# Adding the rounding to a weight piece in two instructions of half the columns

## The chip, the cores and the metric

The kernel runs on one core of a Trainium2 chip. The metric is the device time of one execution in microseconds; the median of three runs before the change is 1360.98 us (1359.57 to 1361.94). A core has five engines that work side by side, each through its own queue in order: TensorE (PE, with its weight load PEld), VectorE (DVE), ScalarE (ACT), GpSimd (POOL) and SyncE (SP), which here issues the DMAs. They meet through semaphores.

## The reference

An attention block with normed queries and keys is followed by a two-layer network. The weights come as float64.

```python
q_n, k_n = rmsnorm(q, g_q), rmsnorm(k, g_k)          # (8, 12, 448, 64)
scores = (1/8) * q_n @ k_n.T
attn = softmax(scores)
x = (attn @ v) as (8*448, 768)
h = x @ w_in                                         # w_in (768, 2048), float64
out = (h - tanh(h)) @ w_out                          # w_out (2048, 768), float64
```

## The kernel before, in words

The 48 steps of attention (8 batches by 6 pairs of heads) are interleaved on TensorE with the matmuls of the network: `run(ns)` draws as much network work out of a generator as fits a gap between two stages of an attention step. The order of every queue is the order in which the Python code issues its instructions; nothing is reordered later. The network's products are formed by a scheme with seven products for eight blocks, which needs sums and differences of weight blocks.

Weights are float64 and are used as float32. They come in 32 pieces of 128 partitions by 768 values (`PIECES`; pieces 0 to 15 of w_in, 16 to 31 of w_out). A piece goes through these stages:
- load, by `weight_load` (lines 287 and 291, on SP): both 32-bit words of each value go to a raw buffer. The first eight pieces use space of the tile gT; from the ninth on there are three buffers named w_raw, so the load of a piece waits until the third piece before it has been finished.
- a, `round_weight_a` on ScalarE (lines 71 and 72): the high word becomes an absolute value in another scale; the low word is scaled in place.
- b, `round_weight_b` on VectorE (lines 78, 79 and 82): a clamp, a shift pair, and the sign bit.
- c, `round_weight_c` on GpSimd (line 90): the scaled low word is added to the bits, as an integer add, which does the rounding.

`weight` does stage a of the next piece and, through `settle`, b and c of the one before, then issues loads. It is called from the slots of the first batch and from inside the products of the first batch (`due` says which piece must be ready for which product). After every fourth piece of w_in, `combine_weights` lists four sums, which `combine` runs on VectorE (line 354) one at a time; they read whole pieces. `keep_weights` and `keep_w_out` store pieces and sums to DRAM for the later batches (lines 369 and 385, on SP). All 32 pieces have been through stage c after about 230 us.

Other lines named below: 140, 141 and 142 are the norm of a query and key pair (reduce and scale on VectorE, power on GpSimd); 454 and 452 scale the queries; 465 and 469 are transposes on TensorE; 567 the scores; 573 the exponentials; 694 the sums of the exponentials and 699 their reciprocal on VectorE; 621, 671 and 633 the products with v; 763 divides; 791 (GpSimd, sometimes VectorE) forms differences of x; 839 the matmuls of a product in the seven-product scheme; 906 to 922 combine products on ScalarE and VectorE; 886 and 887 are tanh and the subtraction of it (887 on GpSimd or VectorE); 1256 the matmuls of the second layer for the first batch, in which matmul f reads row block f of w_out, and a piece holds two such blocks, 384 columns each; 1049 (GpSimd) forms differences of g for later batches.

Of the kernel before, what the change touches and what calls it, by code (L numbers as in the profile page):

```python
# [13 lines left out]
ALU = mybir.AluOpType  # L14
# [72 lines left out]
def round_weight_c(nc, raw, dst):  # L87

    bits = dst.bitcast(I32)
    nc.gpsimd.tensor_tensor(out=bits, in0=bits, in1=raw[:, :, 0], op=ALU.add)  # L90


def fetch(nc, name, t, pair, in_order=False):
# [51 lines left out]
def bounded_path(tc, ctx, q, k, v, moe_w_in, moe_w_out, out, g_col, ident, ones, half_ones, neg_half, early):  # L145
# [192 lines left out]
    def finish_weights(to):  # L338
        while done[2] < to:
            round_weight_c(nc, raws.pop(done[2]), weight_dst(done[2]))  # L340
            done[2] += 1
            if done[2] % 4 == 0 and done[2] <= CF:
                combine_weights(done[2] // 4 - 1)
            keep_w_out(done[2] - 2)
# [1455 lines left out]
```

## Time and profile before

| | |
|---|---|
| median of three runs | 1360.98 us |
| the profiled execution | 1361.07 us |
| its span, first to last instruction | 1359.3 us |
| mean granted TensorE clock | 0.996 |
| PE, DVE, ACT, POOL busy | 1318.1, 956.4, 557.4, 762.9 us |
| L90 (32 instructions) | 17.1 + 9.2 + 41.0 us, 1.83 to 2.69 us each |
| L354 (16 instructions) | 0.95 to 2.61 us each |

The profile is of one execution. A line such as "L90 POOL ... 59.34 2.58" in a timeline is an instruction of line 90 on GpSimd that started 59.34 us after the span's start and took 2.58 us as recorded; the recorded time includes time in which the started instruction was held up. "A <- B" in the list of waits means that an engine sat idle before A until B ended. A busy share is an average over stages with different limits; what a change in one stage is worth is read from that stage.

### The profile page before, as it was taken

The page shows a single profiled execution, that of the slowest core. Times are in us where ns is not written, and L with a number is a line of the kernel's source. Part 1 is how long each engine was busy: PE and PEld are TensorE (multiplying, and loading weights), DVE is VectorE, ACT ScalarE, POOL GpSimd, SP SyncE. Part 2 cuts the span into 40 slices and gives each one's busy share as a digit, 9 for nine tenths or more (in the row PEclk, how much of TensorE's full clock was granted, in tenths as well). Part 3 has the DMA queues.
Part 4 walks back from the last instruction along what each step waited for, and adds up shares of the span by engine and source line. Part 5 has one row for each costly group of instructions (what it writes and reads, how often), then busy time and mean ns, then how long its engine had stood idle before and what let it go on. Part 6 is the DMA issues. An engine that isn't in the chain of part 4 may idle for free.

```text
span 1359.3 us, 29138 instructions
## 1 busy us (share of the span) xinstructions
PE 1318.1 (97%) x11336; PEld 1028.3 (76%) x11336; DVE 956.4 (70%) x1393; ACT 557.4 (41%) x1326; POOL 762.9 (56%) x559
## 2 busy tenths in 40 slices
PE   7988999999999999999999999999999999999996
PEld 3466854478998888687788787778787888699984
DVE  5999989756865677587887576768786668433553
ACT  7855654244343454445322446354512254211100
POOL 4756665347846246726698235843699153712760
PEclk9999999999999999999999999999999999999998
DMA  7878889879999766466555867475645865365544
GB/s 172 189 201 251 265 257 240 251 247 284 324 290 278 184 159 177 111 184 158 162 143 139 201 165 179 108 179 163 167 140 137 166 193 163 94 171 181 165 140 79
DMA packets 371687, 253.53 MB, mean 187 GB/s; under 512 B 282196, under 2 KB 310228, under 8 KB 371540
## 3 DMA queue, kind: packets, MB, share of 16 engines
q1 hardware_dynamic: 371536, 251.57, 67.2%
q8 instruction: 92, 1.51, 0.5%
q14 instruction: 55, 0.45, 0.1%
q10 hardware_dynamic: 4, 0.00, 0.0%
HBM read 205.23 MB, written 46.27 MB: 185 GB/s over the span
## 4 chain that ended last, share of the span: by engine, by line
PE 82%; DVE 10%; DMA 2%; SPq 2%; issue 1%; ACT 1%; POOL 1%; DVEq 0%; ACTq 0%; POOLq 0%
PE mm L839 35%; PE mm L1092 23%; PE sc L567 8%; PE sc L633 6%; PE mm L1256 5%; DVE xT L760 2%; DMA w_raw<-in_moe_w_in_dram 1%; PE sc L671 1%; DVE rows L611 1%; PE sc L621 1%; DVE rows L604 1%; DVE rows L598 1%; DVE sum_T L708 1%; SPq L125 1%; SPq L287 1%
## 5 line engine op out<-in xcount | busy, mean ns | idle before, releaser
L839 PE MATMUL mm<-xT,w_f 128*128 128x224 f32 x1296 | 264.0, 353 | 1.1 <-DVE s L910 0.7
L839 PEld LDWEIGHTS mm<-xT,w_f 128*128 128x128 f32 x1296 | 244.4, 190 | 7.2 <-issue 5.5
L567 PE MATMUL sc<-qT,kT 64*32 64x448 f32 (+1 forms) x3072 | 213.3, 498 | 2.7 <-ACT p_last L573 1.5
L839 PE MATMUL mm<-tt,w_f 128*128 128x224 f32 x1044 | 213.7, 356 | 0.6
L839 PEld LDWEIGHTS mm<-tt,w_f 128*128 128x128 f32 x1044 | 194.9, 190 | 18.9 <-issue 15.6
L521 POOL TENSOR_TENSOR rr_mine<-rr_mine,neg_half 128x28 f32<-128x28 f32 x33 | 160.6, 4866 | 2.8
L756 DVE TENSOR_TENSOR xT<-xT,sc 128x448 f32<-128x448 f32 x32 | 19.9, 621 | 177.6 <-PE sc L567 119.4
L1092 PE MATMUL mm<-u,w_f 128*128 128x224 f32 x672 | 136.5, 354 | 1.2 <-DVE sum_all L731 1.0
L887 POOL TENSOR_TENSOR gT<-s,th 128x448 f32<-128x448 f32 x44 | 55.8, 1270 | 144.9 <-ACT th L886 141.7
L1092 PE MATMUL mm<-gT,w_f 128*128 128x224 f32 (+1 forms) x480 | 133.0, 429 | 3.1 <-DVE acc L1099 3.0
L1092 PEld LDWEIGHTS mm<-u,w_f 128*128 128x128 f32 x672 | 126.1, 190 | 8.2 <-POOL u L1049 3.8
L567 PEld LDWEIGHTS sc<-qT,kT 64*32 64x32 f32 x3072 | 70.8, 106 | 70.1 <-issue 51.7
L1092 PEld LDWEIGHTS mm<-gT,w_f 128*128 128x128 f32 x480 | 90.2, 190 | 40.6 <-issue 34.2
L633 PE MATMUL sc<-p,v_nat 64*32 64x448 f32 x1120 | 110.5, 536 | 0.0
L1092 PE MATMUL mm<-g,w_f 128*128 128x224 f32 (+1 forms) x360 | 99.5, 428 | 1.1 <-DVE acc L1099 1.1
L723 ACT COPY sum_g<-sum 32x14 f32<-32x14 f32 x280 | 56.3, 201 | 105.8 <-DVE sum L715 100.1
L573 ACT ACTIVATE p<-sc 128x448 f32<-128x448 f32 x132 | 71.7, 543 | 50.3 <-PE sc L567 42.4
L887 POOL TENSOR_TENSOR g<-s,th 128x448 f32<-128x448 f32 x24 | 30.3, 1265 | 108.5 <-ACT th L886 93.6
L1092 PEld LDWEIGHTS mm<-g,w_f 128*128 128x128 f32 x360 | 67.9, 190 | 28.1 <-issue 26.2
L1256 PE MATMUL mm<-gT,w_out 128*128 128x448 f32 x192 | 74.3, 542 | 0.0
L142 POOL TENSOR_TENSOR rr<-rr,neg_half 112x8 f32<-112x8 f32 (+1 forms) x30 | 49.1, 1667 | 32.7 <-DVE rr L141 32.3
L1049 POOL TENSOR_TENSOR u<-gT 128x448 f32<-128x448 f32 x48 | 59.1, 1252 | 11.1 <-PE mm L1092 11.1
(196 smaller groups left out, 2424.0 us busy)
## 6 DMA issues: line engine op xcount, KB each, us to landing
w_f<-w_in SPq DMA_DIRECT2D x196, 384.0 KB, 3.4
w_f<-w_inner SPq DMA_DIRECT2D x63, 512.0 KB, 3.5
w_f<-w_out SPq DMA_DIRECT2D x42, 512.0 KB, 3.8
w_raw<-in_moe_w_out_dram SPq DMA_DIRECT2D x16, 768.0 KB, 5.5
w_in<-w_out SPq DMA_DIRECT2D x21, 384.0 KB, 5.2
qk_nat<-in_q_dram SPq DMA_DIRECT2D x132, 56.0 KB, 2.9
qk_nat<-in_k_dram SPq DMA_DIRECT2D x132, 56.0 KB, 2.3
g<-w_out SPq DMA_DIRECT2D x14, 512.0 KB, 4.7
```

The source lines that it names most:

```text
L142: nc.gpsimd.tensor_tensor(out=r, in0=r, in1=neg_half[:rows], op=ALU.pow)
L521: nc.gpsimd.tensor_tensor(out=mine, in0=mine, in1=neg_half[:, :1].to_broadcast([P, 2 * NJ]), op=ALU.pow)
L567: nc.tensor.matmul(tiles[h][i * BL : (i + 1) * BL, :n], lhsT=kT[r, c * P + at : c * P + at + BL], rhs=qT[r, first : first + n], start=True ...
L573: nc.scalar.activation(p[:, h, c if c < 2 else 0, :], tiles[h][:, :n], AF.Exp, scale=1.0 if rr is None else rr[:, 0, 2 * c + h : 2 * c + h ...
L633: nc.tensor.matmul(av[g][i * BL : (i + 1) * BL, :S], lhsT=v_nat[keys, h, c, m * BL : (m + 1) * BL], rhs=p[keys, h], start=first, stop=True ...
L723: nc.scalar.copy(out=acc[h * BL : (h + 1) * BL, g], in_=part[g * BL : (g + 1) * BL, h * NJ : (h + 1) * NJ])
L760: nc.vector.tensor_tensor(out=x[rows], in0=x[rows], in1=rs, op=ALU.mult)
L839: nc.tensor.matmul(bank[:, f * HS : (f + 1) * HS], lhsT=w[:, c * width + f, :], rhs=moving[p](c), start=(first and f == 0 and c == 0), sto ...
L887: eng.tensor_tensor(out=g[:, rows, cols], in0=h, in1=th, op=ALU.subtract)
L1049: nc.gpsimd.tensor_tensor(out=u[:, half], in0=a[:, half], in1=z[:, half], op=ALU.subtract)
L1092: nc.tensor.matmul(bank[:, :n], lhsT=w(i), rhs=mv, start=(first and i == 0), stop=(i == len(moving) - 1), skip_group_check=not first,)
L1256: nc.tensor.matmul(bank[:, :S], lhsT=w_out_row(f, n // HC)[:, n % HC * P : (n % HC + 1) * P], rhs=g[:, f, :], start=(f == 0), stop=(f == C ...
```

## The change

Stage c of a piece is issued as two integer adds instead of one, the first over columns 0 to 383 and the second over columns 384 to 767 of the same piece. Values, buffers and the order of all other instructions are the same.

```diff
 def round_weight_c(nc, raw, dst):
 
     bits = dst.bitcast(I32)
-    nc.gpsimd.tensor_tensor(out=bits, in0=bits, in1=raw[:, :, 0], op=ALU.add)
+    half = bits.shape[1] // 2
+    for part in (slice(0, half), slice(half, 2 * half)):
+        nc.gpsimd.tensor_tensor(out=bits[:, part], in0=bits[:, part], in1=raw[:, part, 0], op=ALU.add)
```

## The prediction

> **What bounds the kernel now.** I read the page's head first (PE 97% busy), then the waits of PE, then the busy times by stretch, then the timelines of DVE and POOL. The add on line 90 runs 32 times, all of them between 32.2 and 230.4 us, so only that part matters. Busy time by stretch, columns start:end, length, then PE, PEld, DVE, ACT, POOL busy with instruction counts, granted clock, DMA share, GB/s:
>
> ```profile
> 66.00:72.00 6.00, 5.54 (x80) 2.92 (x84) 5.81 (x9) 2.64 (x6) 5.38 (x6) 0.72 0.94 210
> 72.00:124.00 52.00, 43.26 (x440) 33.49 (x433) 50.95 (x67) 26.63 (x48) 30.68 (x16) 1.00 0.82 234
> 124.00:236.00 112.00, 111.96 (x896) 73.81 (x895) 100.95 (x126) 67.39 (x123) 69.06 (x42) 1.00 0.85 248
> ```
>
> From 72 to 124 us DVE is busy 50.95 of 52 us and PE only 43.26; after 124 PE has no gap (111.96 of 112). What PE waited for between 58 and 126 us (total us, times, longest):
>
> ```profile
> PE mm L839 <- DVE s L908: 4.0, 2, 2.5
> PE sc L465 <- DVE rs L699: 3.9, 2, 2.6
> PE mm L465 <- DVE rs L699: 1.9, 1, 1.9
> PE mm L839 <- DVE s L918: 0.8, 1, 0.8
> PE mm L694 <- DVE xT L763: 0.5, 1, 0.5
> ```
>
> All 11.1 us are waits for DVE, at 64.05, 67.2, 83.9, 90.0, 104.1, 117.7 and 121.0 us; the last ends at 123.61. DVE works its queue in order and has hardly a gap from 54 to 124 us, so a microsecond taken from it before the reciprocal L699 at 122.0 is a microsecond of the kernel, and nothing after 124 or before 54 is. (PE has no gap from 45 to 64 either.)
>
> Part of DVE's busy time is blocking. The timeline around the first piece with sums (start us, us, instruction), POOL and DVE lines together:
>
> ```profile
> 56.04 0.97 POOL L791 TENSOR_TENSOR tt<-xT,tt 128x224 f32<-128x224 f32 x1 [0.56 <-DVE xT L763]
> 56.52 0.91 DVE L79 TENSOR_SCALAR w_out<-w_out 128x768 int32<-128x768 int32 x1
> 56.97 0.98 POOL L791 TENSOR_TENSOR xT<-xT 128x224 f32<-128x224 f32 x1
> 57.46 1.40 DVE L82 SCALAR_TENSOR_TENSOR w_out<-gT,w_out 128x768 int32<-128x768 int32 x1
> 57.91 1.47 POOL L791 TENSOR_TENSOR tt<-xT,tt 128x224 f32<-128x224 f32 x1
> 58.79 1.41 DVE L354 TENSOR_TENSOR w_out<-w_out,w_out 128x768 f32<-128x768 f32 x1
> 59.34 2.58 POOL L90 TENSOR_TENSOR w_out<-w_out,gT 128x768 int32<-128x768 int32 x1
> 60.23 2.51 DVE L354 TENSOR_TENSOR w_out<-w_out,w_out 128x768 f32<-128x768 f32 x1
> 62.66 0.67 DVE L140 TENSOR_REDUCE rr<-n 112x8 f32<-112x512 f32 x1
> ```
>
> Undisturbed, L79 takes 0.56, L82 0.96, L354 0.95, a 224-column POOL subtraction 0.66 and L90 1.83 us. Here each instruction is long by just the rest of the other engine's. The second L354 takes 2.51 because L90 runs till 61.92: its own 0.95 us begin at 61.79. The engines take turns, each handover some 0.12 us before the other's recorded end. Decisive for the change: the POOL subtraction at 56.97 has no wait of its own and stands directly behind the one before, yet L79, waiting since 56.52, got in between.
>
> **What the Trainium skill says.** "SBUF — State Buffer", section "SBUF: two separate sides": DVE and GpSimd share a port pair as an exclusive lock, held for the whole instruction; the loser blocks fully. Its section "Who interferes with whom" says that DVE instructions with two SBUF inputs or in a 2-port mode contend, tensor_reduce and those with one SBUF input don't. The trace agrees: L78, L79, L82 and L354 are stretched (0.56 to 2.10, 0.95 to 2.61), L763 and L908, with one input in PSUM, never (0.39, 0.62). "GPSIMD Engine Reference", section "Instruction dispatch": each instruction pays a dispatch, an indirect call of tens of cycles; the trace prices it below. "TensorE: Matmul & The Clock Gate", section "What's actually happening": the clock halves after an idle window of about 3.4 us that doesn't start with the kernel. Here the granted clock was 0.50 between 68 and 70 us, after the stalls at 64 and 67; the 32 matmuls of L694 then took 3.1 us instead of 1.65.
>
> **The change, part by part.** It replaces each 768-column add by two of 384. Nothing else moves on any engine. GpSimd has 32 instructions more; the second half has almost never a wait of its own. Consumers of a whole piece (sums L354, the reload of the raw buffer on SP, keeps) now wait for the second half; matmuls wait for the half they read.
>
> Length of a half: 224 columns take 0.66 us, 448 take 1.14 (L887), 768 take 1.83: 2.15 ns a column and 0.17 us fixed. A half is 0.17 + 384 x 2.15 ns = 1.00 us; with the 0.04 us that back-to-back POOL instructions overlap, a pair is 1.97, 0.14 more than 1.83. Over 32 pieces that is 4.5 us of POOL time, hidden by POOL's idle time: 21 us in 72 to 124, 43 us in 124 to 236.
>
> What it does to DVE: a contending DVE instruction now waits for at most one half, and the second half waits behind it. That gains only where the DVE instruction after it doesn't contend and hides the second half; where contending ones follow each other, DVE waits for the second half too. I go through the ten pieces in the bound stretch, letting the two take turns with a handover of 0.12 us:
> - 49.6: L141 (a tiny tensor_scalar, stretched to 0.77) waits for a pair that ends 0.12 later: -0.12.
> - 59.3 and 71.4, the same pattern: L354 starts when the first half ends, 0.82 earlier; the second half runs beside the reduce L140, but its tail holds L141 by 0.14 to 0.17: +0.68 each.
> - 83.7: beside L699, which doesn't contend; L78 waits for the later end: -0.14.
> - 87.7 and 91.3: L79/L82 and L78/L79 follow each other; DVE waits once for each half: +0.07 and +0.08.
> - 95.8: L354 0.81 earlier, second half beside L887, tail holds L78: +0.50.
> - 101.8: four L763 beside it, nothing contends: 0.
> - 108.7: L78 then L79, and the POOL subtraction L887 behind: +0.09.
> - 113.5: L354 0.82 earlier, second half beside L140, then the second L141 meets L887: +0.60.
> Sum: -0.12 + 1.36 - 0.14 + 0.15 + 0.50 + 0 + 0.09 + 0.60 = 2.44 us by L699 at 122.0. The piece at 121.4 delays nothing before that.
>
> Can PE and the others follow? Two DVE instructions come close to waiting for PE: L914 (its matmuls end 104.08, it starts 104.66) and L908 (117.7 and 118.54). PE's own shift there is 1.17 and 1.75, against DVE's 1.75 and 2.44, so they tie with 0 and 0.15 us left; no loss, but no more gain. The second halves end up to 1.0 us later. The reload on SP at 98.30 waits for such an end; its data are used by ACT at 105.26, 3.4 us after landing. Queued behind it on SP are a store and the q and k rows for a later pair. The matmuls closest to an add are those of the piece at 187.97: they need its first half at about 190.8 and its second at 191.6; the halves end at about 189.3 and 190.6 (before: 190.13). After 124 us nothing is gained and, with these margins, nothing lost.
>
> Unknowns, from both sides. Handover between the halves: full, 2.44; never, ten times 0.14 lost, +1.4. I take full, because of 56.97. L141's holding: nothing, gain up to 2.9; a whole half at 59 and 71, gain 1.6. Fixed cost of a half: 0.1 to 0.3 us, gain from 2.9 down to 1.7.
>
> Against the profiled execution (1361.07 us, span 1359.3, 1.8 around it): 1361.07 - 2.44 = 1358.6. That execution is 0.09 above the median 1360.98, so the same number stands for both: 1358.6 us, -0.18%. A measurement of this kernel can tell about 0.2% (2.7 us) from no change; the shown runs spread over 2.4 us.
>
> **Rivals.** (a) The clock halves after the last stall. The stalls at 117.7 and 121.0 stay about 4 us together less 0.7; before, the gate didn't fall there. The halved clock at 68 us was hidden by the next stall; behind 123.6 nothing hides it: about 1.5 us (3.1 - 1.65), gain left 0.9, 1360.1. Against: one stall in seven did it. (b) The second half holds the pair against the waiting DVE instruction, so the change doesn't do what it does on paper: +1.4, 1362.4. Against: 56.97 and 57.91. (c) Slower: the weight stream becomes the bound. From 124 us SP waits long for L90 before reloading the three raw buffers, and ACT for the DMA. If each of the four turns of a buffer up to the piece at 187.97 loses 0.9 us and its matmuls wait, with a lead of 2.9 us (its bits were ready at 185.08) and 1.5 us more, it decides from 4.4 us on; at twice 0.9 a turn, 7.2 - 4.4 = 2.8 lost, and with nothing gained 1363.8. Against: four turns at 0.9 are 3.6. (d) More is given back: L141 isn't held, the fixed cost is below 0.17: 3.3 us, 1357.7.
>
> **How the numbers follow.** The main case, 2.44 with bounds 1.6 to 2.9: 0.58; (d) 0.20; (a) 0.12; (b) 0.05; (c) 0.05. With 0.8 us of scatter in a difference of medians, somewhat under half of the main case and most of (d) lie beyond 2.7 us: faster 0.45. Slower is (c) with part of (b): 0.07. The rest, 0.48, is within 0.2%. The main case alone reaches from 1357.3 to 1360.0; 8 times in 10 with the others 1356.9 to 1361.0.
>
> **What would show it.** Right: L90 twice 1.0 us; the L354 at 60.2 at some 1.7 us instead of 2.51; PE's stalls for DVE at about 8.7 us instead of 11.1; the last of them ends near 121.2; the rest from there as long as before. Wrong: L354 still 2.5 us (b), a clock of 0.5 beyond 121 us (a), waits of PE on L90 after 124 us (c).

## The result, and the profile after

The changed kernel takes 1357.89 us (median of 18 runs, 1356.19 to 1361.06), the kernel before, run beside it, 1361.43 (18 runs, 1359.57 to 1363.98). The ratio is 0.9973, 95% interval 0.9966 to 0.9980: 3.7 us faster (2.7 to 4.6), or 0.27%. The forecast was a gain of 2.4 us, just under what can be told from no change. The time lies in the predicted range and in the main case's own range (1357.3 to 1360.0), but the measured gain is larger than the working gave: 2.4 lies below its interval. The profiled execution took 1356.19 us, with a span of 1354.4 against 1359.3 before.

The head of the page after, busy time of each engine:

```profile
span 1354.4 us, 29206 instructions
PE 1317.9 (97%) x11336; PEld 1029.0 (76%) x11336; DVE 949.1 (70%) x1393; ACT 556.9 (41%) x1326; POOL 775.1 (57%) x591
```

DVE has as many instructions as before (1393) and is busy 7.3 us less (956.4 before): its instructions do the same, so what went is time in which they were held. POOL has the 32 instructions more and is busy 12.2 us longer, where the working priced the 32 at 4.5. Most of the rest is time in which halves were held in their turn (up to 1.87 us each where the shortest took 1.00).

The same three stretches as in the prediction (start:end, length, PE, PEld, DVE, ACT, POOL busy with instruction counts, granted clock, DMA share, GB/s), of the kernel after:

```profile
66.00:72.00 6.00, 5.54 (x113) 2.84 (x116) 5.80 (x9) 3.35 (x8) 5.39 (x6) 1.00 1.04 231
72.00:124.00 52.00, 45.10 (x419) 36.51 (x410) 49.39 (x67) 28.28 (x50) 33.40 (x25) 0.97 0.84 236
124.00:236.00 112.00, 112.00 (x885) 72.48 (x884) 98.18 (x129) 64.95 (x120) 77.01 (x61) 1.00 0.88 251
```

From 72 to 124 us PE is busy 45.10 us instead of 43.26, partly because the clock, 1.00 there before, was at 0.5 for 3.4 us from 91.8 us on. What PE waited for between 45 and 126 us (total, times, longest), after:

```profile
PE sc L467 <- DVE rs L701: 3.9, 2, 2.3
PE mm L841 <- DVE s L910: 2.5, 1, 2.5
PE mm L467 <- DVE rs L701: 1.0, 1, 1.0
PE mm L841 <- DVE rs L701: 0.5, 1, 0.5
PE mm L696 <- DVE xT L765: 0.5, 1, 0.5
```

That is 8.4 us instead of 11.1, again all for DVE (lines after the edited one are numbered two higher). The last of these stalls ends at 120.83 instead of 123.61 us. This is the predicted picture, 8.7 us and about 121.2, a little better.

The piece that the prediction took for its example, DVE and POOL lines of the timeline after, together (start us, us, instruction):

```profile
58.90 3.11 DVE L356 TENSOR_TENSOR w_out<-w_out,w_out 128x768 f32<-128x768 f32 x2
59.48 3.43 POOL L92 TENSOR_TENSOR w_out<-w_out,gT 128x384 int32<-128x384 int32 x2
61.94 0.67 DVE L142 TENSOR_REDUCE rr<-n 112x8 f32<-112x512 f32 x1
62.65 0.29 DVE L143 TENSOR_SCALAR rr<-rr 112x8 f32<-112x8 f32 x1
```

Consecutive like instructions stand on one line. The two sums take 3.11 us together and not 1.41 + 2.51; taken singly they are 1.43 and 1.65 us, the second from 60.36 on. The reduce follows at 61.94 instead of 62.66. This execution stood 0.12 us behind before it, so the second sum gave 0.84 us (0.82 in the working), and the tiny L143, held to 0.29 us by the second half, took 0.12 of that back. The two halves run from 59.48 to 62.91, where the whole add ran to 61.92: GpSimd now ends later and VectorE earlier. The prediction's price of a half, 1.00 us, is the shortest of the 40 halves of pieces w_out read against the raw buffer (1.001 us, median 1.032, longest 1.866, the long ones held by VectorE).

How VectorE's gain builds up, comparing the two profiled executions instruction by instruction, in us:

| piece at (before) | predicted | measured |
|---|---|---|
| 49.6 | -0.12 | +0.18 |
| 59.3 | +0.68 | +0.72 |
| 71.4 | +0.68 | +0.70 |
| 83.7 | -0.14 | -0.15 |
| 87.7 | +0.07 | +0.13 |
| 91.3 | +0.08 | +0.16 |
| 95.8 | +0.50 | +0.53 |
| 101.8 | 0 | 0 |
| 108.7 | +0.09 | +0.14 |
| 113.5 | +0.60 | +0.65 |
| sum | 2.44 | 3.06 |

The execution after was 0.30 us late on VectorE before any of these pieces, so that at the reciprocal L699 (122.0 us) VectorE is 2.78 us ahead. TensorE is ahead by the same 2.78 us at its last stall, and by 3.04 us at its last matmul (1343.33 us instead of 1346.37). The other 1.85 us of the 4.9 by which the spans differ lie behind the last matmul, in a tail of 11.07 us instead of 12.91. That tail is 9.5 to 13.3 us in the profiled executions of all the kernels below, without order (12.01 and 12.91 where nothing is cut, 13.16 and 9.53 where pieces are cut), so I don't count it as the change's.

### The profile page after: what moved, and what is told of

Read it like the earlier page. It is cut to its first block, busy times and chain, and to the rows that moved or that the text cites. A ratio compares the mean times of both kernels' runs of the same rounds, so it can differ in the third digit from the quotient of the medians.

```text
span 1354.4 us, 29206 instructions
## 1 busy us (share of the span) xinstructions
PE 1317.9 (97%) x11336; PEld 1029.0 (76%) x11336; DVE 949.1 (70%) x1393; ACT 556.9 (41%) x1326; POOL 775.1 (57%) x591
## 4 chain that ended last, share of the span: by engine, by line
PE 84%; DVE 9%; DMA 2%; SPq 2%; issue 1%; ACT 1%; POOL 1%; DVEq 0%; ACTq 0%
PE mm L841 36%; PE mm L1094 23%; PE sc L569 9%; PE sc L635 6%; PE mm L1258 5%; DVE xT L762 1%; PE sc L673 1%; PE sc L623 1%; SPq L955 1%; PE mm L673 1%; DVE rows L613 1%; DMA w_f<-w_in 1%; DVE rows L606 1%; DVE rows L600 1%; DMA w_f<-w_inner 0%
## 5 line engine op out<-in xcount | busy, mean ns | idle before, releaser
L1051 POOL TENSOR_TENSOR u<-gT 128x448 f32<-128x448 f32 x48 | 58.8, 1247 | 11.1 <-PE mm L1094 11.1
```

Of the source, the lines that this page charges most:

```text
L1051: nc.gpsimd.tensor_tensor(out=u[:, half], in0=a[:, half], in1=z[:, half], op=ALU.subtract)
```

## The experiments

The question: does the whole gain come from the ten pieces in VectorE's stretch, by the turns that the two engines take, as the prediction says (the theory)? Or does part of it come from the other 22 pieces, or from something else (the rival)? All kernels have this edit in common, with another list of cuts in each:

```
-def round_weight_c(nc, raw, dst):
+def round_weight_c(nc, raw, dst, n):
     bits = dst.bitcast(I32)
-    nc.gpsimd.tensor_tensor(out=bits, in0=bits, in1=raw[:, :, 0], op=ALU.add)
+    cuts = cuts_of(n)
+    for lo, hi in zip(cuts, cuts[1:]):
+        nc.gpsimd.tensor_tensor(out=bits[:, lo:hi], in0=bits[:, lo:hi], in1=raw[:, lo:hi, 0], op=ALU.add)
```

Here n is the piece, 0 to 31. The ten pieces of the table above are 2 to 11. The ten of the experiments are 3 to 12: without the piece at 49.6, and with the one at 121.4, which by the prediction's reading delays nothing before the reciprocal. Lines behind it are numbered six higher than before (L96 is the add, L360 the sums, L705 the reciprocal). "VectorE" below is by how much its reciprocal at 122.0 us came earlier than in the profile of the kernel before; it is negative where that came later, and two executions differ in it by up to 0.7 us with nothing cut. All gains in time come from the ratio to the kernel before on the same chip, whose medians were 1362.05, 1361.80 and 1361.92 us in the three groups of runs.

### Only the ten pieces in halves

```
+    return (0, 384, 768) if 3 <= n <= 12 else (0, 768)
```

> Only the ten pieces of the stretch in which DVE bounds (pieces 3 to 12, adds between 59 and 124 us) are added in two halves, the other 22 in one instruction. Theory (the gain is DVE time given back in that stretch alone): the last stall of PE for DVE ends some 2.8 us earlier than before and the whole is 2.5 to 3.7 us faster, as with all pieces split. Rival (the finer waits of the later pieces, for matmuls and reloads, give part of it): under 1.5 us.

Measured: 1359.65 us, ratio 0.9983 (0.9974 to 0.9993), 2.3 us faster (1.0 to 3.5). VectorE 2.90 us. The step from instructions to VectorE's lead holds.

### All but the ten pieces

```
+    return (0, 768) if 3 <= n <= 12 else (0, 384, 768)
```

> The other half of the change: pieces 0 to 2 and 13 to 31 in two halves, pieces 3 to 12 in one instruction. Theory: within 0.7 us of before, PE's stalls for DVE at about 11 us as before. Rival (later pieces count): 1 to 2 us faster. Second rival (the later ends of the second halves cost something that the whole change hides): 1 us slower.

Measured: 1359.92 us, ratio 0.9990 (0.9981 to 0.9998), 1.4 us faster (0.3 to 2.6). VectorE -0.13 us, and TensorE's stalls up to 126 us sum to about what they were before (11.3 and 11.1 us). So there is a gain elsewhere, and the rival has a part. The two parts, 2.3 and 1.4, add up to the 3.7 of the change.

### Only four pieces in halves

```
+    return (0, 384, 768) if n in (3, 4, 8, 11) else (0, 768)
```

> Only pieces 3, 4, 8 and 11 are added in two halves: those behind whose add DVE has an instruction that does not contend (a reduce, or a subtraction out of PSUM). Theory (a split gains only where such an instruction hides the second half): 2.6 us by the last stall, nearly all of the gain of all ten. Rival (any split add gives DVE an earlier turn): four tenths of it, about 1.1 us.

Measured: 1359.99 us, ratio 0.9983 (0.9975 to 0.9992), 2.3 us faster (1.1 to 3.4). VectorE 2.55 us. The four pieces at which a sum met the add, and a reduce or other instruction that doesn't contend stood behind it, bring nearly all of the 2.90 that all ten bring, and not the four tenths (about 1.1) of the rival. The gain isn't spread evenly over the pieces.

### The add of the ten pieces left out

```
+    return (0,) if 3 <= n <= 12 else (0, 768)
```

> The add is left out for pieces 3 to 12, so these weights lack the rounding by the low word. What the whole adds cost DVE: theory (blocking by the shared port) 9.5 us of DVE time by the last stall; PE's stalls for DVE were 11.1 us in all, so the whole is 7 to 9.5 us faster, less where DVE or PE then wait for each other. Rival (POOL's adds only happen to stand beside DVE's long instructions): under 3 us, and the sums still up to 2.5 us each.

Measured: 1351.12 us, ratio 0.9918 (0.9905 to 0.9930), 11.2 us faster (9.5 to 12.9). VectorE 9.85 us. This is the whole price of these ten adds, though GpSimd was idle for 21 us from 72 to 124 us. What TensorE waited for between 45 and 126 us in this kernel:

```profile
PE sc L471 <- DVE rs L705: 2.0, 2, 1.1
PE mm L845 <- DVE s L914: 0.6, 1, 0.6
PE mm L700 <- DVE xT L769: 0.5, 1, 0.5
PE mm L471 <- DMA qk_nat<-in_q_dram: 0.4, 1, 0.4
```

3.5 us are left of 11.1. So most of what TensorE waits for in this stretch is VectorE held by the add of its neighbour. Of the 9.85 us on VectorE the change gives back 2.78, under a third.

### Quarters

```
+    return (0, 192, 384, 576, 768)
```

> All pieces in four adds of 192 columns (0.58 us each). Theory (turns; the gain per handover shrinks since each part adds its fixed 0.17 us and the rest of the parts meets the next contending instruction): DVE is 3.2 us earlier at the last reciprocal than before, 0.4 more than with halves; whole 3 to 4 us faster than before. Rival (the finer the better in proportion): 5 us or more.

Measured: 1358.04 us, ratio 0.9974 (0.9964 to 0.9985), 3.5 us faster (2.0 to 4.9). VectorE 2.81 us, no more than with halves; 3.2 was expected, and the scatter of 0.7 is larger than that difference. What VectorE waited for between 54 and 124 us shows a wait that the arithmetic of turns didn't have:

```profile
DVE w_out L360 <- POOL w_out L96: 1.0, 1, 1.0
DVE w_f L360 <- POOL w_f L96: 0.5, 1, 0.5
```

In the timeline, the add and the sum that waits for it (eight quarters of two pieces stand on one POOL line):

```profile
85.38 6.74 POOL L96 TENSOR_TENSOR w_out<-w_out,gT 128x192 int32<-128x192 int32 x8 [1.54 <-ACT qT L479]
...
88.90 1.33 DVE L360 TENSOR_TENSOR w_out<-w_out,w_out 128x768 f32<-128x768 f32 x1 [1.04 <-POOL w_out L96]
```

A sum reads whole pieces. Each part lets one more of VectorE's instructions through, so the last part ends later, and the sum behind it stands idle for that end. The first reader of the whole piece sets a limit to finer cuts here.

### Unequal parts

A quarter of the columns first, and a quarter last:

```
+    return (0, 192, 768)      # small_first
+    return (0, 576, 768)      # big_first
```

> All pieces in two adds of 192 and 576 columns. Theory (turns): the waiting DVE instruction comes in earlier, but the long second part (1.41 us) outlasts the instruction that should hide it and holds the next contending one: 1.9 us by the last stall, 0.9 less than equal halves. Rival (only the time to the first handover counts): 0.4 us at each of ten pieces more than halves, 5 us or more.

> All pieces in two adds of 576 and 192 columns. Theory (turns): 1.3 us by the last stall. Rival (the number of instructions counts, not where the cut is): as with equal halves, 2.8 us.

Measured: small first 1358.65 us, ratio 0.9978 (0.9972 to 0.9985), 3.0 us faster (2.0 to 3.8), VectorE 1.29 us (1.95 counted from 58.8 us on, where this execution stood 0.66 behind); big first 1358.73 us, 0.9977 (0.9969 to 0.9985), 3.1 us faster (2.0 to 4.2), VectorE 1.65 us. On VectorE both are worse than halves. The waiting instruction is held by the first part, and the tiny one after the reduce by what is left of the second part, so neither part may be long. In the times the three can't be told apart.

### The sums later in the slot

Halves as in the change, and the sums moved from the end of a slot to behind the norm's reduces and the reciprocal:

```
         if has(s):
             totals(s, mm_bank())
+        combine(2)
...
             weight(s + 2)
-        combine(2)
```

> Halves, and in the first slots the two sums on DVE stand behind the reduces and the reciprocal of the next pair instead of right behind the sign step, so that the add runs beside instructions that do not contend. Theory (turns): DVE is 3.6 us earlier than before by the last stall, 0.9 more than with halves; whole 3.3 to 4.5 us faster than before. Rival (the sums only move their wait, since the small scale steps between the reduces are held instead): no better than halves, 2.8 us.

Measured: 1356.69 us, ratio 0.9965 (0.9952 to 0.9978), 4.8 us faster than before (3.0 to 6.5), the fastest version here that leaves nothing out (five runs). Beside the changed kernel's own interval (0.9966 to 0.9980) that isn't a safe difference. VectorE 3.41 us. DVE and POOL lines of its timeline at the example piece:

```profile
58.80 0.70 DVE L146 TENSOR_REDUCE rr<-n 112x8 f32<-112x512 f32 x1
59.39 1.99 POOL L96 TENSOR_TENSOR w_out<-w_out,gT 128x384 int32<-128x384 int32 x2
59.54 0.89 DVE L147 TENSOR_SCALAR rr<-rr 112x8 f32<-112x8 f32 x1
60.35 0.67 DVE L146 TENSOR_REDUCE rr<-sq 128x8 f32<-128x512 f32 x1
61.44 1.56 DVE L705 RECIPROCAL rs<-mm 128x224 f32<-128x224 f32 x1
62.92 2.22 DVE L360 TENSOR_TENSOR w_out<-w_out,w_out 128x768 f32<-128x768 f32 x2
```

The add now runs beside the reduces, which don't contend (0.70 and 0.67 us there); a pair takes 1.99 us, and of VectorE's instructions only the tiny L147 is held (0.89 us for 8 columns, the second one 0.36). The sums, which read two inputs in SBUF, come when the add is over. The reciprocal, for which TensorE waits, starts at 61.44 and not behind the sums.

### The same order with whole adds

The move of the last experiment, and:

```
+    return (0, 768)
```

> The sums behind the reduces and the reciprocal as in the run with halves, but every add in one instruction. Theory (turns): a whole add holds the small scale step between the reduces for 1.2 us and ends only there, DVE 0.5 us earlier than before at the last reciprocal, so the whole within 1 us of before: the new order needs the halves. Rival (the order alone brings it): 1.5 us or more.

Measured: 1360.79 us, ratio 0.9995 (0.9985 to 1.0004): no difference. VectorE came 0.32 us later than before. At the example piece the tiny instruction alone now takes what the sums were spared, and the sums don't run undisturbed either (timeline, DVE):

```profile
60.19 1.75 DVE L147 TENSOR_SCALAR rr<-rr 112x8 f32<-112x8 f32 x1
...
64.24 2.52 DVE L360 TENSOR_TENSOR w_out<-w_out,w_out 128x768 f32<-128x768 f32 x2
```

So the order alone brings nothing that can be measured. That it pays with an add in halves fits VectorE's 3.41 us against 2.78, but neither that nor the difference in time is clear of the scatter.

### Cuts chosen piece by piece

The sums later as above; quarters for pieces 3 and 4, thirds for 8, halves for 6, 7, 10 and 11, the rest whole.

```
+    return {3: (0, 192, 384, 576, 768), 4: (0, 192, 384, 576, 768), 6: (0, 384, 768), 7: (0, 384, 768), 8: (0, 256, 512, 768), 10: (0, 384, 768), 11: (0, 384, 768)}.get(n, (0, 768))
```

> The sums behind the reduces, and cuts where they pay: quarters for pieces 3 and 4, halves for 6, 7, 10 and 11, thirds for 8, the rest whole. Theory (turns): DVE 4.4 us earlier than before at the last reciprocal, whole 4 to 5.5 us faster. Rival (with more parts the sums wait for the last part, as with quarters everywhere): no better than halves with the sums later, 3.4 us at the reciprocal.

Measured: 1358.04 us, ratio 0.9977 (0.9968 to 0.9985), 3.2 us faster (2.0 to 4.4), VectorE 3.64 us, where 4.4 was expected. At the example piece, four quarters hold both tiny L147 (0.48 and 0.50 us, undisturbed 0.17), where two halves held the first for long and the second less (0.89 and 0.36). The late pieces are whole here, and the gain in time is no more than VectorE's.

### Nothing cut, and only the late pieces

A control with the loop in place and every piece whole, and the nineteen pieces behind VectorE's stretch in halves:

```
+    return (0, 768)                                     # same_again
+    return (0, 768) if n <= 12 else (0, 384, 768)       # split_late
```

> Every add in one instruction, as in the kernel before: what the comparison gives for no change. Both theories: ratio 1.000 within 0.001, DVE at the last reciprocal within 0.4 us. It says how much of the 1.4 us that the split of pieces 0 to 2 and 13 to 31 alone measured is more than that.

> Only pieces 13 to 31 in two halves. Theory (nothing can be gained after PE has caught up with DVE): within 0.7 us of before. Rival (the later pieces do give 1 us or more, by the finer waits of the matmuls and reloads): 1 to 2 us faster, and a place after 126 us in the trace where PE runs ahead of before.

Measured: the control 1361.59 us, ratio 1.0003 (0.9994 to 1.0012); the late pieces alone 1359.83 us, ratio 0.9984 (0.9976 to 0.9993), 2.2 us faster (1.0 to 3.3), while VectorE was 0.37 us later. So there is a second gain, clear of the control's interval around no change, and it lies behind 124 us, where the prediction had none.

Part of it shows between 215 and 240 us. SyncE's load of a raw piece, ScalarE's first step on it and the exponentials behind that, and TensorE's scores, in the control:

```profile
220.39 0.37 SPq L297 DMA_DIRECT2D w_raw<-in_moe_w_out_dram  x1
226.96 0.95 ACT L71 ACTIVATE w_out<-w_raw 128x768 f32<-128x768 f32 x1 [4.30 <-DMA w_raw<-in_moe_w_out_dram]
229.07 0.78 ACT L579 ACTIVATE p_last<-sc,rr 128x224 f32<-128x224 f32 x2
228.57 1.98 PE L573 MATMUL sc<-qT,kT 64*32 64x448 f32 x16
```

With the late pieces in halves:

```profile
220.06 0.37 SPq L297 DMA_DIRECT2D w_raw<-in_moe_w_out_dram  x1
225.75 0.95 ACT L71 ACTIVATE w_out<-w_raw 128x768 f32<-128x768 f32 x1 [3.33 <-DMA w_raw<-in_moe_w_out_dram]
227.86 0.80 ACT L579 ACTIVATE p_last<-sc,rr 128x224 f32<-128x224 f32 x2
228.34 1.01 PE L573 MATMUL sc<-qT,kT 64*32 64x448 f32 x16
```

And the weight loads of the scores in the control, waiting (226 to 231 us):

```profile
PEld sc L573 <- ACT p_last L579: 0.9, 1, 0.9
```

ScalarE works in order. It stands 4.30 us for a raw piece, and the exponentials p_last behind it, which free the bank that the scores need, come at 229.07; TensorE loses about a microsecond (sixteen matmuls in 1.98 us and not 1.01). With halves ScalarE waits 3.33 us, the exponentials come at 227.86, and TensorE loses next to nothing. Of those 1.21 us, the load was issued 0.33 us earlier and took 0.88 us less until its data were used. 0.23 us of it is no gain: by so much TensorE was further on in this execution already at 225 us. Over all profiled executions, TensorE's loss between 215 and 240 us against the kernel before was 1.2, 1.0, 0.7, 0.4, 0.3 and 0.2 us in the six other kernels with whole late adds, and 0.13, 0.03, 0, 0, 0 and 0 in the six with the late adds in two parts (0.6 with quarters). That is about half a microsecond on average. The profiled execution of the kernel before, on which the prediction rests, is the one with whole adds that lost nothing here.

The rest of the 2.2 us (1.0 to 3.3) I could not find as a place in the traces, and why the loads land sooner wasn't tried. The profiled executions can't give the sum: at its last matmul the one with only the late pieces in halves was 2.5 us behind the kernel before, and the one with all but ten 0.07 us ahead.

The mean granted clock of each run gives a rival for part of it: in this group of runs, those with 0.001 more of it were 0.7 us shorter. With only the late pieces in halves the mean clock was 0.9951, in the kernel before 0.9942. An estimate from these runs, at equal clock, leaves 1.1 us (0.5 to 1.8) of a difference of means of 1.8; for all but the ten it is 1.4 (0.5 to 2.2) of 1.8, with a slope of 0.6 us in that group. Whether the cut raises the clock or these runs just had more of it isn't shown. That, and the cause of the earlier loads, stay open.

### All of them side by side

| kernel | VectorE at 122 us | late pieces | measured gain (95%) |
|---|---|---|---|
| all whole, control | -0.69 | whole | -0.4 (-1.6 to 0.8) |
| sums later, whole | -0.32 | whole | 0.7 (-0.5 to 2.0) |
| four in halves | 2.55 | whole | 2.3 (1.1 to 3.4) |
| ten in halves | 2.90 | whole | 2.3 (1.0 to 3.5) |
| chosen cuts | 3.64 | whole | 3.2 (2.0 to 4.4) |
| ten left out | 9.85 | whole | 11.2 (9.5 to 12.9) |
| all but ten in halves | -0.13 | cut | 1.4 (0.3 to 2.6) |
| only late in halves | -0.37 | cut | 2.2 (1.0 to 3.3) |
| small first | 1.29 | cut | 3.0 (2.0 to 3.8) |
| big first | 1.65 | cut | 3.1 (2.0 to 4.2) |
| the change, halves | 2.78 | cut | 3.7 (2.7 to 4.6) |
| quarters | 2.81 | cut | 3.5 (2.0 to 4.9) |
| sums later, halves | 3.41 | cut | 4.8 (3.0 to 6.5) |

With whole late pieces the gain is VectorE's lead, within the intervals; with cut ones it is that lead and 0.7 to 2.6 us more (0.9 for the change). The same estimate at equal clock brings the ten left out from 11.2 to 9.8 us, VectorE's lead. That is the account of the change: some 2.8 us on VectorE before 122 us, shown by what the ten pieces do, and about 1 us from the late pieces, whose cause is shown only in part.

## Why the prediction was right, and where it was not

**What bounds the kernel.** Right. TensorE's stalls up to 124 us are VectorE's lateness, and what VectorE gains there the kernel gains: with the ten adds left out, 9.85 us on VectorE became 11.2 us (9.5 to 12.9) of time.

**The turns of the two engines.** Right, piece by piece, as the table shows. The Trainium skill ("SBUF — State Buffer", section "SBUF: two separate sides") holds that the lock is kept for a whole instruction. The trace agrees in both directions: a whole add held the second sum to 2.51 us, and two adds back to back let it in between, at 1.65 us. The value chosen for the unknown handover (full) was the right end, and rival (b), that the pair holds together, is excluded by that 1.65.

**The first piece.** For the piece at 49.6 the working had -0.12, because L141 waits for the whole pair, and +0.18 was measured. In the change's execution the add began 0.6 us later than before and the reduce 0.3 us, so the first half was still running at 50.97 us when the tiny instruction (L143 there) came: it got in between the halves and took 0.26 us instead of 0.77, and the second one was held to 0.35. With all but ten in halves, where the add began as before (49.59 us), the tiny instruction did wait for the pair (0.93 us), and the piece cost 0.16 us. So the step was right for the executions that it was worked out from, and the plus here came from how the engines stood, which is luck. The other pieces came out 0.32 us better in sum, and so the term 2.44 was 3.06.

**After 124 us.** This step failed: "After 124 us nothing is gained and, with these margins, nothing lost." The late pieces gain 1.4 us (0.3 to 2.6) with the early three and 2.2 (1.0 to 3.3) alone. The working had looked for a loss by the later end of a pair and found none, rightly. That a pair could bring work forward there wasn't asked, because TensorE had no gap from 124 to 236 us in the one profiled execution. But no gap is not no loss. Matmuls that wait for their weight load are shown as busy: where the control lost its 1.0 us at 228 us, the list of what PE waited for from 200 to 252 us is empty. The execution that the prediction read lost nothing at 228, but it had such a loss elsewhere, in the chain that ended last and in the waits of PEld from 150 to 180 us:

```profile
163.67 1.50 PE sc L567 x16
PEld sc L567 <- ACT p_last L573: 0.5, 1, 0.5
```

The same sixteen matmuls took 0.91 us at 195.66. Against this, the change's execution lost at 133 us (its lead fell from 2.78 to 2.12 us) and had the lead back at 170 us. So time could be gained after 124 us, and the share of busy time, 111.96 of 112, could not say so. The predicted time held all the same, because the range was wide enough for the microsecond that was left out.

**The clock.** Rival (a) set a halved clock behind the last stall against the change. It began between 121 and 126 us in 7 of the 14 profiled executions, the control's among them (124.0 us), and not in the change's, which had its half clock at 91.8 us. It cost 1.5 to 1.7 us at once, where 1.5 was priced, of which 0.5 to 0.7 were left against the kernel before at 180 us. It came in four of the seven executions with whole late pieces and in three of the seven with cut ones, so the profiles show no link to the cut; one execution of each kernel is too few to exclude one.

**The weight stream**, rival (c), didn't come: with only the late pieces in halves the kernel got faster, by 1.0 to 3.3 us. In the change's profile weight loads waited for a half in two places, 0.7 us in all (0.2 us for a whole add of a late piece before). **Rival (d)**, more given back on VectorE, came partly true: 2.78 to 3.06, between the main case and 3.3.

## What to carry to other kernels

Where two engines hold each other up for whole instructions, an instruction costs the neighbour what is left of it when the neighbour's contending instruction comes, and cutting it in two gives back the second part if the instruction behind that one doesn't contend. A few places bring nearly all of that (four of ten pieces here). More parts brought nothing that could be measured, and something that waits for the whole then stood idle. Before "nothing is gained here" is written of a stretch, look at a second execution of the same instructions, and at matmuls that took longer than their like, for a busy engine can be a waiting one.

## What the runs showed of the hardware

- Ten adds on GpSimd, 1.83 us each undisturbed and 18 us together, cost VectorE 9.85 us.
- A tiny VectorE instruction on 8 columns, 0.17 us undisturbed, is held like a long one: 1.75 us beside a whole add, 0.89 us beside halves.
- The pair of GpSimd power instructions behind the norm took 3.24 us with whole adds and the sums later, and 3.96 us in halves and sums later, where the sums ran beside them. It seems to be held by VectorE too; this wasn't tried by itself.
- The granted clock fell to half for 3.4 us (6.8 us twice), now here and now there: once near 67 us before and once near 92 us after; three times with ten pieces in halves, never before the last matmul with small first or with the ten adds left out. It fell after stalls of 2.5 us, but at 67.3 us in the kernel with halves and the sums later it fell after stalls of only 1.1 and 0.5. The last stall before and the last one with quarters, 2.6 us each, had none behind them. In one experiment, where it fell at 125 us (all but ten in halves), the windows show 0.57 of the full clock from 125 to 129 us.
- TensorE counted as busy can be waiting: in the control sixteen matmuls of the scores took 1.98 us, without a gap, where 1.01 us is enough, while their weight loads waited for ScalarE.
- The tail from the last matmul to the end of the span differs by up to 3.8 us between executions (9.5 to 13.3), more than this whole change, so spans of single executions can't price it.
